# Expert weights A loaded in whole rows and laid out by eight 0/1 matmuls, with units 0 and 1 handled singly, in a scan-plus-adapters kernel

## The chip, the cores and the metric

The kernel runs on one core of one Trainium2 chip. The metric is the device time of one execution in microseconds. Before the change the median of five runs is 203.0 us (202.66 to 203.38).

## What is computed

Two stages follow each other. The first is a linear recurrence over 6400 steps in each of 8 batches with 128 channels; the second sends every one of the 51,200 resulting rows through the best two of eight small adapters of rank 16:

```python
for t in range(S):                      # B, S, D = 8, 6400, 128
    h = a[:, t] * h + b[:, t]
    x[:, t] = h
logits = x @ w_gate                     # (51200, 8)
topk = two largest of each row;  w = softmax over these two
out = x + sum over the two experts e of  w_e * ((x @ A[e]) @ B[e])
```

w_gate is 128 x 8, A is 8 x 128 x 16 (expert, channel, rank), B is 8 x 16 x 128. The large arrays are a, b and the output, 26.2 MB each; A and B are 64 KB each.

## The kernel before

**Units.** The 51,200 rows are cut into 100 units of 512 rows. A unit's a and b come in by DMA with rows on partitions and are transposed by PE against an identity (lines 474 to 517, "AB": 16 fp32 transposes for each unit), so that channels lie on partitions and time runs along the free axis. ACT copies the transposed a from PSUM to SBUF (line 526, "aev"). DVE runs the recurrence with one scan instruction per unit (line 550) and writes x in fp16 to a ring of 20 units.

**Adapters.** For each block of 128 rows PE multiplies x with the joined weights of w_gate and all eight A, 136 columns (line 589, "ZL"); ACT copies the result to a ring (line 607, "zl"). For a group of units the gate is worked out from the eight logits on POOL, DVE and ACT (lines 621 to 747); the first and last two groups use a sorting instruction of DVE (line 662), the others two maxima with a masking step between them. POOL multiplies the 128 columns of x A by the gate (line 766, "mul"), PE transposes that back (line 774, "T"), DVE or ACT evacuates it (line 782), PE adds x and the product with B in PSUM (line 802, "D"), and ACT evacuates the output (line 817, "oev"). Stores go out two units at a time (line 834).

**Pairs and single units.** Loads of a and b bring two units at once, with eight consecutive rows on each partition; a few at the edges bring one. A unit's columns are therefore normally read with a stride of eight from a pair of units (`x_block`, line 572), and a product of either unit waits for the scan of the second one (`scanned`, line 579). Units listed in SOLO are read with a stride of four, each needs only its own scan, and their store has 2 KB rows instead of 4 KB (line 840). Before the change SOLO holds only the last two units. The first four groups of the gate are one unit each (`heads`), then three units make a group.

**Who sets the order.** [...] A planner (`_Plan.schedule`, line 89) simulates the five engines and one DMA link with costs written in the code. At each step it takes the operation that can start first; ties go to the smaller due time, which is the unit's number plus an offset of the operation's kind (`KEY`). It also hands out the eight PSUM banks. The result is one fixed list for each engine, with semaphore waits (`run`, line 183). PE, ACT, DVE, POOL and SP (which issues all large loads and stores, in order) each work through their list and wait at the head of it.

**The beginning.** Operations of kind "fix" set up the constants. POOL makes an identity. ACT issues three small loads: w_gate, then B, then A (lines 370 to 394). A must arrive as channel x (expert, rank), while memory holds expert, channel, rank; its load has one run of 16 numbers (64 B) for each expert and channel, 1024 runs. POOL casts each of the three to fp16 (line 430). PE runs ten matmuls of 512 columns on zeros ("heat", line 401) before the first transposes, and two more ("fill", line 411) behind the transposes of each of units 0 to 4. The first products wait for w_gate, for A, and for the scans of units 0 and 1:

```python
deps = [scanned(w) for w in ...] + ["cstg", "cstA"]        # of ZL
def scanned(v):
    return f"scan{v if v in SOLO else v | 1}"
```

Of the kernel before, what the change touches and what calls it, by code (L numbers as in the profile page):

```python
# [5 lines left out]
ALU = mybir.AluOpType  # L6
ACTF = mybir.ActivationFunctionType
F32 = mybir.dt.float32
F16 = mybir.dt.float16
AX = mybir.AxisListType  # L10


CFG = {
    "ring": 8,
    "xr": 20,
    "zr": 48,
    "nout": 24,
    "hold": 20,
    "heads": (1, 1, 1, 1),
    "group": 3,  # L20
    "tails": (2, 2, 1, 1),
    "quick": (2, 2),
    "split": (4, 4),
    "solo": (0, 2),
    "mul": (0, 1, 0, 8),
    "tev": (1, 1, 4, 4),
    "tail": 8,
    "fills": 5,
    "caps": {'a': 3, 'b': 4, 'Z': 1, 'O': 3, 'w': 8},
    "least": {'Z': 1, 'O': 1},  # L30
    "pairs": (98, 2),
# [32 lines left out]
class _Plan:  # L64
# [15 lines left out]
    def add(self, name, eng, kind, unit, busy, emit, deps=(), dma=None, mode=None, takes=(), gives=None):  # L80
        self.ops[name] = _Op(name, eng, kind, unit, busy, self.latency, emit, list(deps), dma, mode, takes, gives)
# [118 lines left out]
def bass_associative_scan_2x2__then__mixture_of_adapters_kernel(  # L200
# [9 lines left out]
    E = moe_w_gate.shape[1]  # L210
    R = moe_A.shape[2]
# [50 lines left out]
    fills, left = [], 0  # L262
# [26 lines left out]
    with ExitStack() as stack:  # L289
        sb = stack.enter_context  # L290

        ident_f = sb(nc.sbuf_tensor("ident_f", [128, 128], F32))
        ident_h = sb(nc.sbuf_tensor("ident_h", [128, 128], F16))
        cst_f = sb(nc.sbuf_tensor("cst_f", [128, E + 256], F32))
        cst_h = sb(nc.sbuf_tensor("cst_h", [128, E + 256], F16))
        warm_t = sb(nc.sbuf_tensor("warm_t", [128, UT], F16))
        warm = sb(nc.sbuf_tensor("warm", [128, 1], F32))
        E_A = E + 128
        wA_h = cst_h[:, 0:E_A]
# [26 lines left out]
        def bank(role):  # L326
            return psum[plan.bank_of[role]]
# [6 lines left out]
        add = plan.add  # L334

        def add_dma(name, eng, unit, starts, slot, ns, deps=(), kind="dma", issue=450.0, after=2000.0):

            if slot not in dma_sem:
                dma_sem[slot] = [sb(nc.semaphore("q_" + "_".join(map(str, slot)))), 0]
            dma_sem[slot][1] += 16 * len(starts)  # L340
            sem, value = dma_sem[slot]

            def emit(h):
                for dst, src in starts:
                    last = h.dma_start(dst, src).then_inc(sem, 16)  # L345
                return last

            add(name, eng, kind, unit, issue * len(starts), emit, deps, (sem, value, ns, after))
# [10 lines left out]
                out=ident_f[:, :],  # L359
                in_=ident_f[:, :],  # L360
                compare_op=ALU.not_equal,
                fill=1.0,
# [6 lines left out]

        add_dma("wg_in", "act", -110, [(cst_f[:, 0:E], moe_w_gate[:, :])], ("wg",), 80.0, (), "fix", 450.0, 2000.0)  # L370
        add_dma(
            "B_in",
            "act",
            -109,
            [(cst_f[:, E + 128 : E + 256], moe_B.rearrange("e r d -> (e r) d"))],
            ("B",),
            220.0,
            (),
            "fix",
            450.0,  # L380
            3500.0,
        )
        add_dma(
            "A_in",
            "act",
            -108,
            [(cst_f[:, E : E + 128].rearrange("d (e r) -> d e r", e=E), moe_A.rearrange("e d r -> d e r"))],
            ("A",),
            700.0,
            (),  # L390
            "fix",
            450.0,
            5500.0,
        )
        add("w0", "dve", "fix", -109, 60.0, lambda h: h.memset(warm[:, :], 0.0))
        add("table", "act", "fix", -107, 1500.0, lambda h: h.activation(warm[:, :], warm[:, :], ACTF.Sigmoid), ["w0"])
        add("wt", "dve", "fix", -109, 60.0, lambda h: h.memset(warm_t[:, :], 0.0))

        def heat(h):
            for _ in range(10):  # L400
                last = h.matmul(bank(("w", -1))[:, :], warm_t[:, 0:128], warm_t[:, :])
            return last

        add("heat", "pe", "fix", -109, 4000.0, heat, ["wt"], mode="half", takes=[("w", -1)], gives=("w", -1))

        def fill(w):


            def emit(h):
                for _ in range(2):  # L410
                    last = h.matmul(bank(("w", w))[:, :], warm_t[:, 0:128], warm_t[:, :])
                return last

            add(f"fill{w}", "pe", "fix", 1000.0, 440.0, emit, [f"AB{w}"], mode="full", takes=[("w", w)], gives=("w", w))

        for w in range(CFG["fills"]):
            fill(w)
        add("idh", "dve", "fix", -108, 230.0, lambda h: h.tensor_copy(ident_h[:, :], ident_f[:, :]), ["id"])
        for name, cols, time, load in (
            ("cstg", slice(0, E), 150.0, "wg_in"),  # L420
            ("cstB", slice(E + 128, E + 256), 400.0, "B_in"),
            ("cstA", slice(E, E + 128), 400.0, "A_in"),
        ):
            add(
                name,
                "pool",
                "fix",
                -108,
                time,
                lambda h, cols=cols: h.tensor_copy(cst_h[:, cols], cst_f[:, cols]),  # L430
                [load],
            )
# [496 lines left out]
```

## Time and profile before

| what | value |
|---|---|
| median of five runs | 203.0 us (202.66 to 203.38) |
| profiled execution | 203.38 us, span of its instructions 201.6 us |
| busy share | PE 90%, PEld 80%, DVE 85%, ACT 89%, POOL 78% |
| moved by DMA | 79.31 MB, mean 393 GB/s over the span |
| first scan starts | 6.09 us |
| second scan | 8.18 to 9.46 us |
| load of A, from issue to landing | 9.2 us (B 3.6, w_gate 3.2) |
| last scan | 182.06 to 183.34 us |
| last store issued | about 196.5 us |

Times inside the profile are microseconds from the start of the span; the difference between 203.38 and 201.6 lies outside it. PE is TensorE's matmuls, PEld its weight loads, DVE VectorE, ACT ScalarE, POOL GpSimd, SP the engine that issues the large DMAs. L550 is line 550 of the kernel. A line of the timeline gives start, length, engine, line, operation, the tile written and those read, the shape, a count, and in brackets how long the engine had been idle and what released it. A line of the stage table gives a stretch of the span, and for each engine its busy time and number of instructions, then the granted TensorE clock, the busy share of the 16 DMA engines and the rate in GB/s. Matmuls overlap, so the busy time of PE is not a measure of useful work.

### The profile page before, as it was taken

To read this page: it belongs to the slowest core of one execution; us is meant where nothing else is said; L and a number is where in the kernel's file an instruction comes from. 1 tells how busy PE (TensorE), PEld (TensorE's weight loads), DVE (VectorE), ACT (ScalarE), POOL (GpSimd) and SP (SyncE) were. 2 spreads that over 40 slices of the span, in tenths; PEclk is the share of its full clock that TensorE was granted. 3 is DMA by queue.
4 is the path that set the end of the run, shared out by engine and by line. 5 is a ranking of instruction groups with operands and counts; after the bars stand their busy time and mean duration, and the time that the engine had idled before them with its cause. 6 is when DMAs were issued, how large, how long until landed. Compare 5 with 4: busy or idle time off the path is not lost.

```text
span 201.6 us, 8187 instructions
## 1 busy us (share of the span) xinstructions
PE 182.1 (90%) x3204; PEld 160.7 (80%) x3204; DVE 171.7 (85%) x296; ACT 179.3 (89%) x461; POOL 157.6 (78%) x280
## 2 busy tenths in 40 slices
PE   7888899998998999989999999989998999997860
PEld 3576788887988988888988898879988989886750
DVE  1489999999899899999879798799797899798950
ACT  2369899998998998998999999999999999999760
POOL 2016568989999797879789899999999999779810
PEclk9999999999999999999999999999999999999997
DMA  5999999999999999999999999999999999988984
GB/s 210 365 406 408 407 406 409 398 414 403 406 419 410 416 413 414 411 411 414 412 412 415 413 411 411 418 411 415 415 413 412 411 410 413 412 350 353 408 317 167
DMA packets 23399, 79.31 MB, mean 393 GB/s; under 512 B 3649, under 2 KB 3777, under 8 KB 23361
## 3 DMA queue, kind: packets, MB, share of 16 engines
q1 hardware_dynamic: 22032, 78.65, 97.4%
q8 instruction: 26, 0.43, 0.9%
q10 hardware_dynamic: 1328, 0.14, 0.5%
q14 instruction: 13, 0.10, 0.1%
HBM read 52.56 MB, written 26.21 MB: 391 GB/s over the span
## 4 chain that ended last, share of the span: by engine, by line
PE 49%; ACT 17%; DVE 12%; DMA 7%; issue 6%; POOL 4%; SPq 3%; DVEq 0%
PE ps L492 18%; PE ps L802 16%; PE ps L589 8%; PE ps L774 8%; DVE xT L550 8%; DMA b_in<-in_b_dram 7%; ACT a_st L526 5%; ACT zl L607 5%; ACT outt L817 4%; SPq L345 3%; POOL zw L766 3%; ACT pn L656 2%; DVE zw L766 2%; DVE zwT L782 1%; ACT g L745 1%
## 5 line engine op out<-in xcount | busy, mean ns | idle before, releaser
L550 DVE TENSOR_TENSOR_SCAN xT<-a_st,xT,ps 128x512 f16<-128x512 f32 x96 | 120.3, 1253 | 12.0 <-ACT a_st L526 5.1
L766 POOL TENSOR_TENSOR zw<-zl,g 128x512 f16<-128x512 f32 x93 | 98.7, 1067 | 7.6 <-ACT g L745 7.6
L607 ACT COPY zl<-ps 128x408 f32<-128x408 f32 (+1 forms) x139 | 71.6, 543 | 0.7 <-PE ps L589 0.5
L492 PE MATMUL ps<-ident_f,a_in 64*128 64x64 f32 (+1 forms) x792 | 67.1, 228 | 4.3 <-DMA b_in<-in_b_dram 1.4
L526 ACT COPY a_st<-ps 128x512 f32<-128x512 f32 x100 | 61.6, 643 | 9.5 <-PE ps L492 8.8
L492 PE MATMUL ps<-ident_f,b_in 64*128 64x64 f32 (+1 forms) x792 | 67.3, 228 | 1.3 <-issue 0.9
L492 PEld LDWEIGHTS ps<-ident_f,a_in 64*128 64x128 f32 (+1 forms) x792 | 56.0, 138 | 14.1 <-issue 4.5
L817 ACT COPY outt<-ps 128x512 f32<-128x512 f32 x99 | 60.8, 630 | 2.7 <-PE ps L802 2.0
L492 PEld LDWEIGHTS ps<-ident_f,b_in 64*128 64x128 f32 (+1 forms) x792 | 55.8, 138 | 1.1 <-issue 0.6
L589 PE MATMUL ps<-cst_h,xT 128*128 128x136 f16 x400 | 49.0, 233 | 1.0 <-issue 0.6
L802 PE MATMUL ps<-ident_h,xT 128*128 128x128 f16 x400 | 42.8, 229 | 2.1 <-issue 1.1
L774 PE MATMUL ps<-ident_h,zw 128*128 128x128 f16 x400 | 38.7, 220 | 3.9 <-DVE zw L766 2.3
L589 PEld LDWEIGHTS ps<-cst_h,xT 128*128 128x128 f16 x400 | 35.5, 148 | 5.0 <-DVE xT L550 0.9
L782 DVE COPY zwT<-ps 128x256 f32<-128x256 f32 x89 | 35.9, 411 | 3.4 <-PE ps L774 3.2
L802 PE MATMUL ps<-cst_h,zwT 128*128 128x128 f16 x400 | 38.7, 219 | 0.0
L802 PEld LDWEIGHTS ps<-ident_h,xT 128*128 128x128 f16 x400 | 33.2, 148 | 4.4 <-DVE zwT L782 1.8
L774 PEld LDWEIGHTS ps<-ident_h,zw 128*128 128x128 f16 x400 | 25.2, 98 | 7.2 <-DVE zw L766 3.2
L802 PEld LDWEIGHTS ps<-cst_h,zwT 128*128 128x128 f16 x400 | 27.2, 99 | 0.0
L656 ACT ACTIVATE pn<-d 128x96 f32<-128x96 f32 (+2 forms) x72 | 23.3, 334 | 0.1
L735 POOL TENSOR_TENSOR um<-d,pn 128x96 f32<-128x96 f32 (+2 forms) x36 | 14.1, 392 | 5.4 <-ACT pn L656 4.8
L706 POOL TENSOR_TENSOR L<-zl,pn 128x96 f32<-128x96 f32 (+2 forms) x34 | 13.4, 395 | 3.8 <-ACT pn L656 3.4
L728 POOL TENSOR_TENSOR d<-d 128x96 f32<-128x96 f32 (+2 forms) x38 | 13.8, 364 | 1.4 <-DVE d L681 0.5
(31 smaller groups left out, 85.9 us busy)
## 6 DMA issues: line engine op xcount, KB each, us to landing
a_in<-in_a_dram SPq DMA_DIRECT2D x49, 512.0 KB, 15.5
b_in<-in_b_dram SPq DMA_DIRECT2D x49, 512.0 KB, 15.5
out_dram<-outt SPq DMA_DIRECT2D x49, 512.0 KB, 15.3
a_in<-in_a_dram SPq DMA_DIRECT2D x2, 256.0 KB, 9.2
b_in<-in_b_dram SPq DMA_DIRECT2D x2, 256.0 KB, 4.4
out_dram<-outt SPq DMA_DIRECT2D x2, 256.0 KB, 4.2
cst_f<-in_moe_B_dram ACTq DMA_DIRECT2D x1, 64.0 KB, 3.6
cst_f<-in_moe_A_dram ACTq DMA_DIRECT2D x1, 64.0 KB, 9.2
```

Of the source, the lines that this page charges most:

```text
L492: last = h.transpose(*args())
L526: lambda h: h.copy(a_st[w % NAS][:, :], bank(("a", w))[:, :]),
L550: last = h.tensor_tensor_scan(out=x_at(lo, hi), data0=a_st[w % NAS][:, lo:hi], data1=bank(("b", w))[:, lo:hi], initial=init, op0=ALU.mult, ...
L589: last = h.matmul(dst, x_block((b0 + j) // Q, (b0 + j) % Q), wA_h)
L607: return h.copy(zl[:, r0 : r0 + n, :], src)
L656: lambda h: h.activation(v(pn[s]), v(src[s]), ACTF.Relu, bias=bias, scale=scale),
L735: lambda h: h.tensor_tensor(out=v(um[s]), in0=v(d1[s]), in1=v(pn[s]), op=ALU.subtract),
L766: lambda h: h.tensor_tensor(out=oview, in0=zview, in1=gview, op=ALU.mult),
L774: last = h.transpose(dst[:, q * 128 : (q + 1) * 128], zw[v % NZW][:, q, :], ident_h[:, :])
L782: return copy(zwT[v % NZT][:, :].bitcast(F32), bank(("O", v))[:, 0 : UT // 2])
L802: last = h.matmul(bank(("O", v))[:, cols], (x_block(v, q), zwT[v % NZT][:, cols])[part], (ident_h[:, :], Bcat_h)[part], start=part == 0 an ...
L817: return copy(outt[:, v % NOUT, :], bank(("O", v))[:, :])
```

## The change

A is now loaded right behind w_gate, ahead of B, with 128 runs of 512 B: partition 16e + h gets the channels 8h to 8h + 7 of expert e, 16 ranks each. To bring this to the layout channel x (expert, rank), each partition's row is spread over eight expert columns, zero in all but its own (multiplied by a mask `mine`, a 0/1 matrix of partition and expert). That is 128 x 1024 products in fp16, three eighths on POOL ("spr0") and five eighths on DVE ("spr1"). Eight matmuls with 0/1 matrices (`pick`, one matrix seen through eight shifted windows) then add into one PSUM bank, each placing 16 channels ("selA"). ACT, instead of POOL, casts the result to fp16 ("cstA"). DVE makes the mask and the 0/1 matrices from the identity in four operations.

Units 0 and 1 become SOLO, so unit 0's products need only its own scan. The heating falls from ten matmuls to six, and the fills from two behind each of five units to two, one and one behind units 0, 1 and 2.

```diff
-    "solo": (0, 2),
+    "solo": (2, 2),
...
-    "fills": 5,
+    "heat": 6,
+    "filler": (2, 1, 1),
...
+        pick = sb(nc.sbuf_tensor("pick", [128, 8 * 129], F16))
+        high = sb(nc.sbuf_tensor("high", [128, 16], F32))
+        mine = sb(nc.sbuf_tensor("mine", [128, E], F32))
+        spread = sb(nc.sbuf_tensor("spread", [128, 8, E, R], F16))
...
         add_dma(
+            "A_in",
+            "act",
+            -109,
+            [(cst_f[:, E : E + 128], moe_A.rearrange("e (h l) r -> (e h) (l r)", l=8))],
...
+            -108,
             [(cst_f[:, E + 128 : E + 256], moe_B.rearrange("e r d -> (e r) d"))],
...
-            [(cst_f[:, E : E + 128].rearrange("d (e r) -> d e r", e=E), moe_A.rearrange("e d r -> d e r"))],
...
-            for _ in range(10):
+            for _ in range(CFG["heat"]):
...
+        add("pick0", "dve", "fix", -109, 330.0, lambda h: h.memset(pick[:, :], 0.0))
...
+                out=high[:, :], in_=ident_f[:, :].rearrange("p (e h) -> p h e", e=E), axis=AX.X, op=ALU.max
...
+            lambda h: h.tensor_copy(
+                pick[:, :].rearrange("p (k c) -> p k c", c=129)[:, :, 0:128:8],
+                high[:, :].unsqueeze(1).broadcast_to([128, 8, 16]),
+            ),
...
+                out=mine[:, :], in_=ident_f[:, :].rearrange("p (e h) -> p e h", e=E), axis=AX.X, op=ALU.max
...
+        for name, eng, lo, hi, time in (("spr0", "pool", 0, 3, 900.0), ("spr1", "dve", 3, 8, 760.0)):
...
+                lambda h, lo=lo, hi=hi: h.tensor_tensor(
+                    out=spread[:, lo:hi, :, :],
+                    in0=raw[:, lo:hi, :].unsqueeze(2).broadcast_to([128, hi - lo, E, R]),
+                    in1=mine[:, :].unsqueeze(1).unsqueeze(3).broadcast_to([128, hi - lo, E, R]),
+                    op=ALU.mult,
+                ),
+                ["A_in", "mine"],
...
+        def gather(h):
+            for k in range(8):
+                last = h.matmul(
+                    bank(("w", -2))[:, 0:128],
+                    pick[:, k * 128 : (k + 1) * 128],
+                    spread[:, k, :, :].rearrange("p e r -> p (e r)"),
+                    start=k == 0,
+                    stop=k == 7,
+                )
+            return last
+
+        add("selA", "pe", "fix", -107, 700.0, gather, ["pick", "spr0", "spr1"], mode="full", takes=[("w", -2)])
+        add(
+            "cstA",
+            "act",
...
+            lambda h: h.copy(cst_h[:, E : E + 128], bank(("w", -2))[:, 0:128]),
+            ["selA"],
...
-                for _ in range(2):
+                for _ in range(CFG["filler"][w]):
...
-            ("cstA", slice(E, E + 128), 400.0, "A_in"),
```

More of the change, by code (lines that the diff above doesn't have):

```diff
@@ L371, in bass_associative_scan_2x2__then__mixture_of_adapters_kernel @@
         add_dma(
+            "A_in",
+            "act",
+            -109,
+            [(cst_f[:, E : E + 128], moe_A.rearrange("e (h l) r -> (e h) (l r)", l=8))],
+            ("A",),
+            220.0,
+            (),
+            "fix",
+            450.0,
+            2500.0,
+        )
+        add_dma(
             "B_in",
             "act",
-            -109,
+            -108,
             [(cst_f[:, E + 128 : E + 256], moe_B.rearrange("e r d -> (e r) d"))],
@@ L380, in bass_associative_scan_2x2__then__mixture_of_adapters_kernel @@
             450.0,
[L381 to L386, printed above, removed]
-            [(cst_f[:, E : E + 128].rearrange("d (e r) -> d e r", e=E), moe_A.rearrange("e d r -> d e r"))],
[L388 to L393, printed above, removed]
+            2500.0,
         )
@@ L399, in heat @@
         def heat(h):
-            for _ in range(10):
+            for _ in range(CFG["heat"]):
                 last = h.matmul(bank(("w", -1))[:, :], warm_t[:, 0:128], warm_t[:, :])
             return last
-        add("heat", "pe", "fix", -109, 4000.0, heat, ["wt"], mode="half", takes=[("w", -1)], gives=("w", -1))
+        add("heat", "pe", "fix", -109, 430.0 * CFG["heat"], heat, ["wt"], mode="half", takes=[("w", -1)], gives=("w", -1))
+        add("pick0", "dve", "fix", -109, 330.0, lambda h: h.memset(pick[:, :], 0.0))
@@ new lines, in bass_associative_scan_2x2__then__mixture_of_adapters_kernel @@
+        add(
+            "high",
+            "dve",
+            "fix",
+            -108,
+            220.0,
+            lambda h: h.tensor_reduce(
+                out=high[:, :], in_=ident_f[:, :].rearrange("p (e h) -> p h e", e=E), axis=AX.X, op=ALU.max
+            ),
+            ["id"],
+        )
+        add(
+            "pick",
+            "dve",
+            "fix",
+            -108,
+            220.0,
+            lambda h: h.tensor_copy(
+                pick[:, :].rearrange("p (k c) -> p k c", c=129)[:, :, 0:128:8],
+                high[:, :].unsqueeze(1).broadcast_to([128, 8, 16]),
+            ),
+            ["pick0", "high"],
+        )
@@ new lines, in bass_associative_scan_2x2__then__mixture_of_adapters_kernel @@
+        add(
+            "mine",
+            "dve",
+            "fix",
+            -108,
+            220.0,
+            lambda h: h.tensor_reduce(
+                out=mine[:, :], in_=ident_f[:, :].rearrange("p (e h) -> p e h", e=E), axis=AX.X, op=ALU.max
+            ),
+            ["id"],
+        )
+        raw = cst_f[:, E : E + 128].rearrange("p (l r) -> p l r", r=R)
+        for name, eng, lo, hi, time in (("spr0", "pool", 0, 3, 900.0), ("spr1", "dve", 3, 8, 760.0)):
+            add(
+                name,
+                eng,
+                "fix",
+                -108,
+                time,
+                lambda h, lo=lo, hi=hi: h.tensor_tensor(
[3 more added lines that the diff above has]
+                    op=ALU.mult,
+                ),
+                ["A_in", "mine"],
+            )
@@ new lines, in gather @@
+        def gather(h):
[6 more added lines that the diff above has]
+                    stop=k == 7,
+                )
+            return last
+        add("selA", "pe", "fix", -107, 700.0, gather, ["pick", "spr0", "spr1"], mode="full", takes=[("w", -2)])
+        add(
+            "cstA",
+            "act",
+            "fix",
+            -107,
+            160.0,
+            lambda h: h.copy(cst_h[:, E : E + 128], bank(("w", -2))[:, 0:128]),
+            ["selA"],
+            gives=("w", -2),
+        )
@@ L406, in fill @@
         def fill(w):
             def emit(h):
-                for _ in range(2):
+                for _ in range(CFG["filler"][w]):
                     last = h.matmul(bank(("w", w))[:, :], warm_t[:, 0:128], warm_t[:, :])
                 return last
-            add(f"fill{w}", "pe", "fix", 1000.0, 440.0, emit, [f"AB{w}"], mode="full", takes=[("w", w)], gives=("w", w))
-        for w in range(CFG["fills"]):
+            add(f"fill{w}", "pe", "fix", 1000.0, (430.0 if w == 0 else 220.0) * CFG["filler"][w], emit, [f"AB{w}"], mode="full", takes=[("w", w)], gives=("w", w))
@@ L417, in bass_associative_scan_2x2__then__mixture_of_adapters_kernel @@
+        for w in range(len(CFG["filler"])):
             fill(w)
```

## The prediction

> **What bounds the kernel now.** I read four views in this order: the chain of work that ended last, the busy table by stages, the timeline of the first 16 us, and the end. The chain (start, length, what) leaves the DMA queue only once:
>
> ```profile
> 6.60 13.78 DMA b_in<-in_b_dram
> 20.37 0.04 issue
> 20.42 0.73 PE ps L492 x16
> 21.17 0.55 ACT a_st L526
> ```
>
> Up to 20.4 us the chain is the load stream; the transfer of b for units 10 and 11 lands at 20.4. After that no transfer is on the chain; it runs through PE, ACT and DVE to the last store. The busy table by stages says how full the engines are (columns: PE, PEld, DVE, ACT, POOL busy us, granted clock, DMA share, GB/s):
>
> ```profile
> 5.39:12.87 7.48, 6.14 (x77) 4.00 (x76) 5.04 (x6) 3.12 (x7) 0.29 (x1) 1.00 1.05 383
> 12.87:20.25 7.38, 6.35 (x112) 5.22 (x112) 6.85 (x19) 7.25 (x22) 4.15 (x11) 1.00 1.03 410
> 20.25:21.17 0.92, 0.75 (x18) 0.69 (x19) 0.92 (x4) 0.01 (x2) 0.39 (x2) 1.00 0.98 392
> 20.00:180.00 160.00, 152.64 (x2830) 138.72 (x2830) 146.11 (x239) 153.96 (x393) 140.61 (x239) 1.00 1.02 410
> ```
>
> From 20 to 180 us ACT is busy 153.96 of 160 us and idle only 6.0; PE 152.64; and the DMA engines are saturated as well, at 410 GB/s. Two limits lie close together. Which is ahead can be read from landings: b of units 98 and 99 is issued at 158.7 and lands 15.5 later, at 174.2, while unit 98 is scanned at 180.2. The shortest such lag, at unit 10, is 22.1 - 20.4 = 1.7 us, so compute trails the loads by some 4 us at the end. Compute, ACT first, sets the end, with the DMA 4 us behind it. So the change can gain in two ways: loads that land sooner in the first 20 us, and engine work done in the idle time before 20 us. Between 5.39 and 12.87 us ACT is idle for 7.48 - 3.12 = 4.36 us.
>
> Why it is idle is in the timeline:
>
> ```profile
> 10.92 0.29 POOL L430 CAST cst_h<-cst_f 128x128 f16<-128x128 f32 x1 [5.80 <-DMA cst_f<-in_moe_A_dram]
> 11.66 0.39 ACT L607 COPY zl<-ps 128x272 f32<-128x272 f32 x1 [0.28 <-PE ps L589]
> 13.23 0.25 POOL L672 TENSOR_TENSOR d<-zl,mx 128x32 f32<-128x32 f32 x1 [2.02 <-DVE mx L662]
> 15.42 1.06 POOL L766 TENSOR_TENSOR zw<-zl,g 128x512 f16<-128x512 f32 x1 [1.41 <-ACT g L745]
> ```
>
> Scan 1 is over at 9.46, but A lands at 10.86; the first product starts at 11.3 and the first gate multiply at 15.42.
>
> **A in 512 B rows.** The present load is 8 x 128 runs of 64 B. Its price shows in the stages it crosses (same columns) and in the queue's packets from 5 to 7 us:
>
> ```profile
> 5.00:6.00 1.00, 1.00 (x10) 0.71 (x8) 0.00 (x0) 0.59 (x1) 0.12 (x1) 1.00 1.13 270
> 6.00:7.00 1.00, 0.79 (x10) 0.57 (x8) 0.91 (x1) 0.00 (x0) 0.00 (x0) 1.00 1.14 328
> 7.00:8.00 1.00, 0.65 (x8) 0.51 (x6) 0.31 (x1) 0.59 (x1) 0.00 (x0) 1.00 1.03 403
> q10 hardware_dynamic: 976, 0.06, 33.9%
> ```
>
> Against 403 GB/s the two stages lose (133 + 75) KB = 0.208 MB, or 0.52 us of the whole DMA. The new A has the shape of B's load, 128 rows of 512 B. From 3 to 4 us the rows of w_gate and B on the same queue, 0.05 MB, took 20.9% of the engines, 0.21 us where 403 GB/s would take 0.12; so some 0.1 us is lost again and I take 0.4 back for every transfer queued behind, b of unit 1 first (lands 7.4, then 7.0). The ends are 0.2 (if other traffic filled part of those stages badly anyway) and 0.5. Landing: B, issued second at 1.18, took 3.6 us; A now has that place, so 4.8 instead of 10.9. B moves to third place: some 5.3, and nobody needs it before the first delta at 17.75.
>
> **What A must pass on the chip.** pick0, high, pick and mine go to DVE. The fill of warm_t took 0.27 for 512 f16, so pick0 about 0.55; the cast of ident_h 0.23, so the other three 0.25 each: 1.3 us, between 1.5 and 4.8, where DVE has nothing until 6.09. Hidden; it would cost only if it passed A's landing at 4.8. spr1 on DVE is 640 elements: the multiply of line 766 takes 0.67 for 512 alone and 1.08 while POOL multiplies too, so 0.84 to 1.35; spr0 on POOL runs beside it (1.06 x 384/512 = 0.8), so I take 1.35: done at 6.2. selA, 8 matmuls: like line 774 (four in 0.40, 0.06 apart), 0.64, so 7.0; cstA on ACT 0.25 (a 128x272 copy has 0.39). A is ready at about 7.4 against 11.2. Queued behind these: scan 0 stands behind spr1 on DVE, 6.2 instead of 6.09; but scan 1 waits for b of unit 1, 7.0 plus 0.65 of transposes, so scan 0 may start as late as 6.5 before anything is late. cstB on POOL waits behind spr0, which nobody feels. The transposes of unit 1 may stand behind selA on PE: 0 to 0.2. ACT's next copy stands behind cstA, 0.25 in idle time.
>
> **Units 0 and 1 single.** Products of unit 0 need scan 0 alone (over at 7.4) instead of scan 1: with A at 7.4 the first copy of zl comes at about 7.9 (11.66 now), the first gate multiply some 3.7 us sooner, about 11.7. Without the early A this part would give nothing, since A ends last. The first store has 2 KB rows instead of 4 KB; at most some 0.1 us at 41 us, taken as nothing.
>
> **Fewer warming matmuls.** Here the Trainium skill speaks against the change. The rows of the weight loads before each warming matmul:
>
> ```profile
> 3.33 0.15 PEld L401 LDWEIGHTS ps<-warm_t 128*128 128x128 f16 x1 [0.28 <-issue]
> 3.76 0.15 PEld L401 LDWEIGHTS ps<-warm_t 128*128 128x128 f16 x1 [0.28 <-issue]
> 4.11 0.31 PEld L401 LDWEIGHTS ps<-warm_t 128*128 128x128 f16 x2 [0.20 <-issue]
> ```
>
> The step is 0.43 us up to 3.76, then 0.35, then 0.2: the array doubles its speed at about 4.1 (the granted-clock row says 1.0 throughout and does not show it). "TensorE: Matmul & The Clock Gate", section on the HAM clock gate, says that half rate lasts until a window of about 3.4 us has been busy. Six matmuls end at 1.22 + 6 x 0.43 = 3.8, before the step in the trace. By the rule, if PE's small gaps then let a window pass, AB0, selA and AB1 last up to twice as long: 0.5 us on scan 1. By the row, a of unit 0 (landed at 3.84, transposed only from 4.54, behind the heating) follows without a gap, and the clock rises as before. I take 0; the ends are -0.1 (unit 0 sooner) and +0.5. The fills fall from ten to four matmuls; PE waits for loads there anyway: 0, at best 0.4 where a fill stands between two products at 11.46.
>
> **Sum.** Loads: -0.4. ACT work that moves ahead of 12.87: two of the four zl copies of units 0 and 1 (2 x 0.39), two relus and two sigmoids (4 x 0.24), less cstA 0.25: 1.5 us. The ends: -0.25 (all of it comes back) and 2.4 with one evacuation of zwT (0.37) and of outt (0.59) as well. Not all is kept: at 20.25 ACT runs dry for 0.92 us, waiting for unit 10, and work done early widens that hole unless deltas of units 1 to 4, now 3.7 us sooner, fill it. POOL's gating of units 2 and 3 takes 6 us (17.98 to 23.76), so they come just in time; I keep half, 0.75. In all -1.15 us. Profiled, 203.38 (span 201.6 and 1.78 around it) would become 202.2; that run is the slowest of the five, and against the median of 203.0 it is 201.85, say **201.9**.
>
> **The rivals.** (1) Only the loads count: the head start is lost in ACT's wait before unit 10, which then reads 1.7 to 2.4 instead of 0.92: 203.0 - 0.4 = 202.6. For it: the chain leaves DMA only at 20.4. Against: POOL idles for several us between 13 and 30, and is what early gating feeds. (2) All of it is kept: 203.0 - 0.4 - 2.2 = 200.4. For it: MoE work runs some twelve units behind when scan 99 ends, so any lead shortens the end. The DMA floor allows it: at 412 GB/s the stages below and their neighbours leave gaps of 1.5 us from 176 to 186 and 1.35 from 194 to 198, so 203.0 - 0.4 - 2.85 = 199.8.
>
> ```profile
> 180.00:182.00 2.00, 1.96 (x25) 1.75 (x23) 1.92 (x5) 2.00 (x7) 2.00 (x5) 1.00 0.72 283
> 194.00:196.00 2.00, 1.85 (x29) 1.50 (x27) 0.59 (x2) 1.78 (x5) 0.00 (x0) 1.00 0.61 237
> ```
>
> (3) Slower: the planner writes a fixed order for every engine from its own costs and due times; with other first ops it writes another one for all 100 units. With ACT idle 6.0 and PE 7.4 of 160 us, an order that makes each of them stall a third more costs 2 us there; less 1.15 that is 203.9. From 1.15 us of added ACT idle between 20 and 180 it decides. Against it: sums, deps and due times of units 2 to 97 are the same, and nothing in the trace points to a worse order rather than a better one.
>
> **How the numbers follow.** Forecast 0.43 (201.3 to 202.5), loads alone 0.20 (202.3 to 202.9), all kept 0.15, new order 0.22. A difference of 0.2%, 0.4 us, is about what a measurement of this kernel tells from none. Faster: 0.41 + 0.10 + 0.15 = 0.66; within: 0.02 + 0.10 + 0.04 = 0.16; slower 0.18. The range 200.4 to 203.9 leaves out half of case 2 and half of case 3, 0.18.
>
> **What would show it.** A's last packet before 5.3 and no stage from 5 to 7 us under 350 GB/s (loads); the first zl copy near 7.9 and the first gate multiply near 11.7 (A's path); b of unit 10 landing near 20.0; ACT busy from 12.87 to 20.25 still over 7 us (kept) or a wait of over 1.5 us before unit 10 (rival 1); ACT idle from 20 to 180 near 6.0 (over 7.2: rival 3). I am wrong if A's path passes 11 us, or if PE still steps at 0.43 us after 6 us.

## The result and the profile after

The changed kernel takes 202.4 us in the median of its runs, against 203.17 for the kernel before in the same sessions: a ratio of 0.9966 (95% interval 0.9952 to 0.998), 0.7 us faster. The profiled execution took 201.97 us, with a span of 199.9 (before 203.38 and 201.6). Ratios leave out executions more than 1.5% above the fastest of their kernel; the profiles of runs o1 and o2 below are of such executions.

The start went nearly as worked out. From the timeline of the changed kernel (PEld is the weight load ahead of the matmuls of the same line):

```profile
4.62 0.83 DVE L454 TENSOR_TENSOR spread<-cst_f,mine 128x640 f16<-128x640 f32 x1 [2.06 <-DMA cst_f<-in_moe_A_dram]
4.67 1.47 POOL L454 TENSOR_TENSOR spread<-cst_f,mine 128x384 f16<-128x384 f32 x1 [0.68 <-DMA cst_f<-in_moe_A_dram]
6.28 0.58 PEld L571 LDWEIGHTS ps<-ident_f,a_in 64*128 64x128 f32 x8 [0.66 <-DMA a_in<-in_a_dram]
6.92 0.62 PE L465 MATMUL ps<-spread,pick 128*128 128x128 f16 x8
7.58 0.27 ACT L481 CAST cst_h<-ps 128x128 f16<-128x128 f32 x1
8.31 0.72 ACT L686 COPY zl<-ps 128x272 f32<-128x272 f32 x2 [0.47 <-PE ps L668]
11.36 1.06 POOL L845 TENSOR_TENSOR zw<-zl,g 128x512 f16<-128x512 f32 x1 [0.72 <-ACT g L824]
```

A lands at 4.6 and is in its layout at 7.85; the first copy of zl comes at 8.31 (11.66 before), the first gate multiply at 11.36 (15.42). What became of this lead is in the stage table, with the stretches of the prediction:

```profile
5.39:12.87 7.48, 6.64 (x101) 4.77 (x100) 5.87 (x16) 4.25 (x13) 2.61 (x5) 1.00 1.02 411
12.87:20.25 7.38, 5.62 (x105) 4.87 (x103) 6.76 (x12) 5.95 (x18) 2.91 (x10) 1.00 1.02 407
20.00:180.00 160.00, 151.89 (x2814) 137.74 (x2812) 145.26 (x237) 153.18 (x390) 140.80 (x240) 1.00 1.02 411
```

ACT (fourth busy time) is 1.67 us ahead at 12.87: 1.13 in the stretch (4.25 against 3.12), and 0.54 of its first copy that already lies ahead of 5.39. It has lost 1.30 again by 20.25 (5.95 against 7.25), since it now runs dry earlier: b of units 8 and 9 lands at 17.4 and PE waits for it.

```profile
17.45 0.27 PE L571 MATMUL ps<-ident_f,a_in 64*128 64x64 f32 x1 [1.61 <-DMA b_in<-in_b_dram]
```

Before the change this hole stood at b of units 10 and 11, and what goes with it shows in the DMA queues. Loads of two units land some 1.3 us apart, but one of them comes late: b of units 10 and 11 landed 2.7 us after their a before the change (17.7, then 20.4), b of units 8 and 9 lands 2.8 us after theirs now (14.6, then 17.4). The queues from 17 to 18.5 us before, and from 14.5 to 16 us after, both hold this:

```profile
q8 instruction: 1, 0.02, 4.5%
```
```profile
q8 instruction: 1, 0.02, 4.5%
```

One packet of 16 KB of instructions, begun at 17.24 (then 14.59), kept one of the 16 DMA engines for 1.1 us; a load has landed only with its last part, so that engine's part would hold it up. Such a packet goes with the longest step (1.6 to 2.9 us) of the loads that land from 10 to 24 us in all fourteen profiles; that it causes the step was not tested.

Between 20 and 25 us ACT, 4.88 busy instead of 4.08, regains 0.8 and stands 1.2 us ahead. The loads gave no such lead: scan 10 starts at 22.2 in both kernels. Then ACT loses that lead far from the change, between 60 and 100 us (kernel before first, then changed):

```profile
60.00:100.00 40.00, 37.52 (x715) 34.47 (x712) 37.30 (x61) 37.64 (x93) 33.34 (x54) 1.00 1.03 413
```
```profile
60.00:100.00 40.00, 36.35 (x685) 33.17 (x686) 36.21 (x58) 36.10 (x90) 33.84 (x56) 1.00 1.03 415
```

ACT does 1.54 us less there. So the last copy to the output tile ends at 196.5 us before and 196.7 after: compute gained nothing in this pair of executions. The 1.7 us of span came from what follows that copy, the landing of the last store (before, then after):

```profile
DMA to landing us min/median/max: 4.5/4.5/4.5
```
```profile
DMA to landing us min/median/max: 2.7/2.7/2.7
```

That is not the DMA engines as a whole. The stage table before (first two lines) and after:

```profile
198.50:199.00 0.50, 0.00 (x0) 0.00 (x0) 0.00 (x0) 0.00 (x0) 0.00 (x0) 0.58 0.42 152
199.00:200.50 1.50, 0.00 (x0) 0.00 (x0) 0.00 (x0) 0.00 (x0) 0.00 (x0) 0.50 0.10 40
```
```profile
198.50:199.00 0.50, 0.00 (x0) 0.00 (x0) 0.00 (x0) 0.00 (x0) 0.00 (x0) 1.00 0.80 311
199.00:199.90 0.90, 0.00 (x0) 0.00 (x0) 0.00 (x0) 0.00 (x0) 0.00 (x0) 1.00 0.00 0
```

Most of the 16 engines were done sooner before the change than after it. But from 199.0 to 200.5 their share was 0.10: one or two engines went on, and a store has landed only with its last part. The queues from 196.5 to 199 before the change have the same kind of packet again, 16 KB of instructions, begun at 196.95 and 1.38 us long:

```profile
q8 instruction: 1, 0.02, 3.4%
```

After the change there is none between 186.4 and 199. So in this pair the gain in span is that no DMA engine is late at the end, and neither the early A nor ACT's lead. It is not only chance: the median span of the recorded executions is about 201.4 before and 200.1 after. Whether the packet falls alike in all of them is not recorded, and it is not the only thing that makes an engine late: in run e7 below one engine goes on from 198.0 to 199.2 (share 0.06) with no such packet after 185.6.

### The profile page after: what moved, and what is told of

Same layout as the page of the kernel before. It is cut to its first block, busy times and chain, and to the rows that moved or that the text cites. A ratio compares the mean times of both kernels' runs of the same rounds, so it can differ in the third digit from the quotient of the medians.

```text
span 199.9 us, 8186 instructions
## 1 busy us (share of the span) xinstructions
PE 181.0 (91%) x3202; PEld 160.6 (80%) x3202; DVE 174.3 (87%) x302; ACT 179.7 (90%) x463; POOL 158.5 (79%) x278
## 4 chain that ended last, share of the span: by engine, by line
PE 50%; DVE 14%; ACT 14%; DMA 8%; issue 6%; SPq 3%; POOL 2%; POOLq 1%; DVEq 0%; ACTq 0%
PE ps L571 18%; PE ps L881 16%; DVE xT L629 10%; PE ps L668 9%; DMA a_in<-in_a_dram 8%; PE ps L853 7%; ACT a_st L605 5%; ACT zl L686 4%; SPq L350 3%; ACT outt L896 3%; DVE zwT L861 2%; ACT pn L735 2%; DVE zw L845 1%; POOLq L290 1%; ACT g L824 1%
## 5 line engine op out<-in xcount | busy, mean ns | idle before, releaser
L686 ACT COPY zl<-ps 128x408 f32<-128x408 f32 (+1 forms) x139 | 74.8, 545 | 1.0 <-PE ps L668 0.8
L571 PE MATMUL ps<-ident_f,a_in 64*128 64x64 f32 (+1 forms) x792 | 68.3, 229 | 5.0 <-DMA b_in<-in_b_dram 2.1
L605 ACT COPY a_st<-ps 128x512 f32<-128x512 f32 x100 | 62.4, 643 | 9.1 <-PE ps L571 8.2
L571 PE MATMUL ps<-ident_f,b_in 64*128 64x64 f32 (+1 forms) x792 | 68.1, 229 | 2.0 <-issue 1.8
L571 PEld LDWEIGHTS ps<-ident_f,a_in 64*128 64x128 f32 (+1 forms) x792 | 56.7, 139 | 15.4 <-issue 4.6
L896 ACT COPY outt<-ps 128x512 f32<-128x512 f32 x100 | 62.0, 636 | 3.5 <-PE ps L881 2.8
L571 PEld LDWEIGHTS ps<-ident_f,b_in 64*128 64x128 f32 (+1 forms) x792 | 56.4, 139 | 1.2 <-issue 1.1
L668 PE MATMUL ps<-cst_h,xT 128*128 128x136 f16 x400 | 49.9, 233 | 0.7 <-DVE xT L629 0.5
L881 PE MATMUL ps<-ident_h,xT 128*128 128x128 f16 x400 | 42.1, 228 | 1.0 <-DVE zwT L861 0.8
```

The source lines that it names most:

```text
L571: last = h.transpose(*args())
L605: lambda h: h.copy(a_st[w % NAS][:, :], bank(("a", w))[:, :]),
L668: last = h.matmul(dst, x_block((b0 + j) // Q, (b0 + j) % Q), wA_h)
L686: return h.copy(zl[:, r0 : r0 + n, :], src)
L881: last = h.matmul(bank(("O", v))[:, cols], (x_block(v, q), zwT[v % NZT][:, cols])[part], (ident_h[:, :], Bcat_h)[part], start=part == 0 an ...
L896: return copy(outt[:, v % NOUT, :], bank(("O", v))[:, :])
```

## The experiments

Two theories were put to the test. **Theory 1**: the change works through its own parts, loads that land sooner and a head start of ACT. **Theory 2**: the fixed lists that the planner writes anew set the time, the start little. All ratios are against the kernel before, run in the same session.

**A's rows alone, all lists kept.**

```diff
-            [(cst_f[:, E : E + 128].rearrange("d (e r) -> d e r", e=E), moe_A.rearrange("e d r -> d e r"))],
+            [(cst_f[:, E : E + 128], moe_A.rearrange("e (h l) r -> (e h) (l r)", l=8))],
```

> The kernel before with one edit: A is loaded in 128 rows of 512 B straight into its tile, and nothing sorts it, so the adapters use wrongly placed weights (the layout of A is left out). The planner's costs are untouched, so every engine's list stays as it was. Theory 1 (the loads that land sooner are worth about 0.4 us, and an early A adds a part of the head start): A is cast by about 6 instead of 10.9, no stage from 5 to 7 us under 350 GB/s, b of units 10 and 11 lands near 20.0; time 0.4 to 0.8 us under before. Theory 2 (the new order of the lists, not the loads, made the gain): within 0.2 us of before, since the lists are the same and ACT waits for the same loads later on.

Measured: 202.76 us, ratio 0.9974 (0.9956 to 0.9992), 0.5 us faster as theory 1 has it, but not by its steps. In the profiled execution A, still issued third, is cast at 7.95, and the loads were later, not sooner (b of units 10 and 11 at 20.9; 304 to 328 GB/s from 5 to 7 us). The early A brought nothing that the profile shows: the first product starts at 11.63 (11.31 before) and the last copy to the output tile ends at 196.56 (196.51). What made the 0.5 us stays open.

**The parts, each with lists of its own.** A's path without the rest; single units without the rest; both with the old heating and fills; the change without single units.

```diff
 e2:  after.py with  "solo": (0, 2), "heat": 10, "filler": (2, 2, 2, 2, 2)
 e3:  before.py with "solo": (2, 2)
 e4:  after.py with  "heat": 10, "filler": (2, 2, 2, 2, 2)
 s1:  after.py with  "solo": (0, 2)
```

> The new A path alone: units 0 and 1 stay a pair, ten heating matmuls and two fills behind each of five units as before. Theory 1: A ready near 7.5, the first products after scan 1 near 9.5 instead of 11.3; about two thirds of the gain, 0.4 to 0.6 us under before. Theory 2: anywhere from 0.7 us faster to 0.7 us slower, since the lists are written anew.

> The kernel before with units 0 and 1 made single and nothing else. A still lands at 10.9, after scan 1, so theory 1 expects nothing: within 0.2 us of before. Theory 2: anywhere from 0.7 us faster to 0.7 us slower, since the lists are written anew.

> The change without its third part: the new A path and single units 0 and 1, with the heating and fills of before. Theory 1: the heating and fills are worth at most 0.1 us, so 0.6 to 0.8 us under before, as the whole change. Theory 2: again an order of its own, so from 0.7 faster to 0.7 slower, not tied to the whole change's 0.7.

> The change without single units 0 and 1: the new A path, six heating matmuls, fills of two, one, one. Theory 1: A is ready at 7.5 and waits for scan 1 at 9.3, so a third of the head start goes; 0.2 to 0.5 us under before. Theory 2: an order of its own, anywhere between 1.9 us under and 3 us over before.

Measured: e2 1.0065 (1.0037 to 1.0092); e3 1.0005 (0.9979 to 1.003); e4 1.0157 (1.0121 to 1.0193); s1 1.0005 (0.9958 to 1.0053). Theory 1 misses e2 and e4 and fits e3; s1's interval, 0.9 us under to 1.1 over, holds its 0.2 to 0.5 under as well as no gain, and decides nothing. Theory 2 has the right kind of effect, but its 0.7 us to either side was too little for e2 (1.3 slower) and e4 (3.2). e4 is the telling one: its start is as good as the changed kernel's (unit 10 is scanned at 22.0 us, against 22.2), and yet it is 3 us slower than before. It loses most of the time between 100 and 140 us, where the kernel before has ACT busy for 39.32; e4:

```profile
100.00:140.00 40.00, 36.71 (x678) 33.53 (x678) 35.61 (x57) 37.35 (x97) 33.70 (x58) 1.00 1.03 415
```

e3's profiled execution (205.47 us, the slowest of its runs, whose median is 203.04) shows what a late A costs when a list wants it early. A landed at 13.7, 12.0 us after its issue where the same load took 9.2 in the profile of before, and PE stood still from 12 to 14 us and then ran at about half the clock (granted clock, third column from the end):

```profile
12.00:14.00 2.00, 0.00 (x0) 0.00 (x0) 1.36 (x2) 0.08 (x1) 0.29 (x1) 1.00 1.04 420
14.00:16.00 2.00, 1.97 (x22) 1.42 (x22) 0.37 (x4) 0.77 (x2) 0.00 (x0) 0.62 1.02 408
16.00:18.00 2.00, 2.00 (x20) 1.12 (x20) 1.08 (x1) 1.20 (x4) 0.70 (x3) 0.53 1.03 412
```

**Order alone.** One number that only the planner sees, the time after which A is taken to have landed. It executes nothing, but moves one early operation in the plan; all five lists come out different, and most operations get another PSUM bank.

```diff
 before.py, A_in:  5500.0 -> 5600.0 (o1), 4500.0 (o2)
 after.py,  A_in:  2500.0 -> 2400.0 (o3), 2600.0 (o4), 2000.0 (o5)
```

> The kernel before with one number of the planner changed, nothing that the chip executes: it takes A to land 0.1 us later (5600 for 5500 ns). The lists that come out differ in most places on all five engines. Theory 1 (the order does not matter, sums and loads do): within 0.2 us of before. Theory 2 (each new order is worth its own stalls): up to 1 us to either side, by ACT idle time between 20 and 180 us that appears far from the start.

> As the run before it, with A taken to land 1.0 us sooner in the planner alone (4500). Theory 1: within 0.2 us of before. Theory 2: up to 1 us to either side, and not the same as the other order.

> The changed kernel with one number of the planner changed: A taken to land 0.1 us sooner (2400 for 2500 ns). Everything that the first 10 us hold is the same work. Theory 1: 0.7 us under before, as the change. Theory 2: the gain of the change is its order's as much as its own, so between 0.7 us under the change and 3 us over it.

> The changed kernel with A taken to land 0.1 us later in the planner alone (2600). Theory 1: 0.7 us under before. Theory 2: an order of its own again, different from the run before it by more than 0.4 us.

> The changed kernel with A taken to land 0.5 us sooner in the planner alone (2000 for 2500 ns), a third other order of the same work. Theory 1: 0.7 us under before. Theory 2: another value between 1.9 us under and 3 us over before; it is also a try at an order that beats the best so far.

Measured:

| run | ratio to before | 95% interval |
|---|---|---|
| o1 | 1.0463 | 1.0386 to 1.0541 |
| o2 | 1.0213 | 1.014 to 1.0286 |
| o3 | 0.9904 | 0.9874 to 0.9934 |
| o4 | 1.003 | 1.0 to 1.0061 |
| o5 | 1.0274 | 1.0209 to 1.0339 |

Theory 2 holds, and by more than it asked for: the same work in another order is worth from 1.0% under to 2.7% over in o3 to o5. Their starts are near the changed kernel's (A lands in 3.4 to 3.6 us, ACT is busy for 10.8 to 12.1 us of the first 20, against 12.0). o1 and o2 lose about as much or more, but perhaps not by order alone: in their profiles A took 12.3 and 11.9 us to land, as in e3, and scan 10 starts at 26.4 and 27.1 instead of 22.2. In o1 that is not the list's doing: up to the first products its lists are those of before. How much of 4.6% and 2.1% is the late A is open. So the start is not always little: e3's profile, with such an A, is 2.4 us over e3's median. Planner inputs 5400 and 5000 give the lists of 5500, with other PSUM banks in part, so the step is sudden. In the profiles ACT's idle time from 20 to 180 us is 5.8 us in o3, 6.0 before, 6.8 in the changed kernel and 9.2 in o5. o3, at 201.59 us in the median, beats both kernels; 0.8 us under the change, by nothing but its order and banks.

**Inside the changed order.** The next two leave every list as in the changed kernel.

```diff
 e6:  after.py, in heat():
-            for _ in range(CFG["heat"]):
+            for _ in range(10):
 e7:  after.py, in A_in:
-            [(cst_f[:, E : E + 128], moe_A.rearrange("e (h l) r -> (e h) (l r)", l=8))],
+            [(cst_f[:, E : E + 128].rearrange("d (e r) -> d e r", e=E), moe_A.rearrange("e d r -> d e r"))],
```

> The changed kernel with ten heating matmuls issued instead of six, while the planner still counts six, so every list keeps its order. Theory 1 (the heating itself costs): the transposes of unit 0 stand 0.5 us later, scan 0 with them, but scan 1 waits for its load anyway; within 0.2 us of the changed kernel, 0.5 to 0.9 us under before. Theory 2 (order): also within 0.2 us of the changed kernel, and then the 3.3 us that the run with the old heating and fills cost against before is its order's. A time over before would say that the heating itself was it.

> The changed kernel with A loaded in 64 B runs again into the same tile, everything else and every list as in the changed kernel; the values that the 0/1 matmuls sort are then wrongly placed (the layout of A is left out). A lands at 9 to 14 us instead of 4.6, in a list that stands scan 0 and the transposes of unit 1 behind it. Theory 1: the early A is what the changed order lives on; 3 to 8 us over before. Theory 2, that A's early landing is worth little and the order is all: within 1 us of the changed kernel.

Measured: e6 202.36 us, ratio 0.9925 (0.9895 to 0.9954), by its median the changed kernel's time (before was slower in that session, 203.57): the heating is worth nothing either way, and e4's loss is not the heating's. e4 has five fill operations where the change has three; what it lost is put down to its lists, which was not tested apart from the fills. e7 202.86 us, ratio 0.9962 (0.9936 to 0.9989), also the changed kernel's. But e7 did not do what it was made for: A was not late. The lines of the DMA table, the changed kernel, then e7, e1 and the kernel before (last column: us from issue to landing):

```profile
cst_f<-in_moe_A_dram ACTq DMA_DIRECT2D x1, 64.0 KB, 3.4
```
```profile
cst_f<-in_moe_A_dram ACTq DMA_DIRECT2D x1, 64.0 KB, 3.8
```
```profile
cst_f<-in_moe_A_dram ACTq DMA_DIRECT2D x1, 64.0 KB, 6.2
```
```profile
cst_f<-in_moe_A_dram ACTq DMA_DIRECT2D x1, 64.0 KB, 9.2
```

In 64 B runs but issued second, A lands in 3.8 us; in 512 B rows but issued third, in 6.2. Its place ahead of B does more than its rows (2.8 and 5.4 us against 0.4 and 3.0), and e7's b of units 10 and 11 lands at 20.0 as well. What a late A would cost in the changed order was not tried.

e6 also shows the limit at the end. There ACT keeps its lead (busy 37.46 from 60 to 100 us), and the last copy ends at 194.6, 2.2 us sooner than in the changed kernel's profile, with the same lists. Its span is still 200.6, since the last store then takes 5.5 us to land:

```profile
DMA to landing us min/median/max: 5.5/5.5/5.5
```

From 197.0 to 199.5 the share of the DMA engines is 0.10, so again one or two engines of 16 are late; 16 KB of instructions were read at 194.2. The end is the later of two: compute's last copy with some 2.3 to 2.7 us for a store that waits for nobody (e4 and e3, whose last copies end at 200.3 and 200.2: 2.3 and 2.6), or the DMA engine that is furthest behind.

## Why the prediction was right, and where it was not

The sign was right, and 0.7 us lies between "only the loads" (0.4) and the forecast (1.15). That the number came near is in part luck: in the profiles neither term reached the end. Step by step:

- **Loads, -0.4.** Unit 10's b lands at 20.0 as said (20.4), and 371 and 385 GB/s replace 270 and 328 from 5 to 7 us. Its cause was half wrong: the early landing is mostly A's place in the queue, not its rows. And it was not passed on: scan 10 starts at 22.2 as before, and the last scan at 183.4 instead of 182.1.
- **A's path.** Ready at 7.85 for 7.4. The spreading was done by 6.14, as said (6.2), though its price was laid on the wrong engine (POOL's share took 1.47, not 0.8, DVE's 0.83, not 1.35; see the last section). The delay is PE's: the sum let the transposes of unit 1 stand behind selA; they stand ahead of it and waited for their load until 6.28, so selA began at 6.92. Scan 0 starts at 5.70, and scan 1 is not held up by it.
- **Warming.** The doubling of the array's speed came later in this profile than the 4.1 of before: the four transposes of unit 0's a take 1.06 us instead of 0.60, those of b likewise; those of unit 1 take 0.71 at 6.28, as before at 6.43. The clock-gate rule of the Trainium skill ("TensorE: Matmul & The Clock Gate", section on the HAM clock gate) has it after a busy window of about 3.4 us; here it came 2.9 us after the first matmul before the change, sooner than that, and 4.2 to 5.1 us after it now. The six heating matmuls need not be the reason: with ten, e1 shows 1.06 for a too, and with six, o3 shows 0.60 for b. Hidden, as taken.
- **Head start, -0.75 kept of 1.5.** ACT is 1.67 us ahead at 12.87, of which 0.27 is the new cast: 1.4, as said. At 25 it is 1.2, so 0.9 kept. The hole that was feared before unit 10 opened before unit 8. What the sum had wrong comes after it: it let the lead run through 160 us to the end. In the profiled execution stalls between 60 and 100 us ate it; in e6, with the same lists, they did not, and the time was the same.
- **What bounds the end.** "Compute sets the end, with the DMA 4 us behind it" was read from the loads, and holds for most DMA engines. It left out the last store's own landing, 4.5 us where an unqueued one takes 2.7, in the same trace: one or two engines ended 1.8 us after the others. That term was put at nothing, and it is what differs between the two profiles.
- **New order.** Rival 3 was priced at 2 us with 0.22. Its mechanism is real and larger: o5, whose start is as good as the change's, is 2.7% over before, 5.6 us. The rule given, that over 1.15 us of added ACT idle between 20 and 180 decides, was not put to the test by the change, which added 0.8.

What part of 0.7 us is the change's own and what its order's stays open. One kernel was measured with the old list and the new rows (0.5 us faster), and of four orders of the changed work two are faster than before, one is slower, and one (o4) cannot be told from it. Mean effects over many orders were not measured.

## What to carry to other kernels

When a planner writes fixed lists for all engines, an edit at the start draws a new order for the whole run: measure several draws, by nudging one of the planner's inputs, before giving a gain or a loss to the edit, and keep the best draw. A lead at the start is worth its size only if nothing behind it is the bound; look at how long the last store takes to land, and at how many DMA engines are still busy then, before trusting a chain that ends in compute. A small load that others wait for can gain more from its place in the queue than from its shape.

## What the runs showed of the hardware

The DMA rate between 60 and 140 us is 412 to 414 GB/s in the five kernels without the four new tiles (before, e1, e3, o1, o2) and 414 to 415 in the nine with them, whatever their order, heating, single units or rows of A. Over 150 us that is about 0.7 us of DMA time, but no profile shows that it reaches the end: most engines were done sooner before the change than after it. The new tiles move the later tiles to other addresses; whether that is the cause was not tried.

When DVE and POOL multiply at the same time, the one that starts second is slowed in the cases looked at. In the changed kernel POOL's spreading starts 0.05 us after DVE's and takes 1.47 us, DVE's 0.83. In o4, where the two do not overlap, they take 0.84 and 0.80:

```profile
4.73 0.84 POOL L454 TENSOR_TENSOR spread<-cst_f,mine 128x384 f16<-128x384 f32 x1 [0.80 <-DMA cst_f<-in_moe_A_dram]
6.52 0.80 DVE L454 TENSOR_TENSOR spread<-cst_f,mine 128x640 f16<-128x640 f32 x1
```

In the kernel before it is the other way round: POOL's gate multiply starts first, and DVE's takes 1.08 us instead of 0.67 alone. From this line the prediction took it that DVE pays.

```profile
184.89 1.06 POOL L766 TENSOR_TENSOR zw<-zl,g 128x512 f16<-128x512 f32 x1
185.41 1.08 DVE L766 TENSOR_TENSOR zw<-zl,g 128x512 f16<-128x512 f32 x1
187.93 0.67 DVE L766 TENSOR_TENSOR zw<-zl,g 128x512 f16<-128x512 f32 x1
```
